# A band mask moved into the score product: sliding-window attention with an MLP gate on one Trainium2 core

## The chip, the cores and the metric

The kernel runs on one core of a Trainium2 chip. The core has five engines with queues of their own: PE (TensorE, matrix products, with a separate row PEld for its weight loads), ACT (ScalarE), DVE (VectorE), POOL (GpSimd) and SP (SyncE, which here only issues DMAs). The metric is the device time of one execution in microseconds; lower is better.

## The reference, cut to what matters

`S` = 2048 tokens, `D` = 512, 32 heads of width 16. Each token attends to itself and to the seven tokens at distances 2, 4, ..., 14 before it.

```python
xn = layernorm(x)
q, k, v = split(xn @ wqkv)                      # 32 heads of 16
off = arange(8) * 2                             # W = 8, dil = 2
idx = pos[:, None] - off[None, :];  mask = idx >= 0
logits = einsum("bhsd,bhswd->bhsw", q, k[idx]) * 16 ** -0.5
attn = softmax(where(mask, logits, -1e9))
s = einsum("bhsw,bhswd->bhsd", attn, v[idx]).reshape(B, S, D) @ wo
h = gelu(layernorm(xn) @ w1);  x1 = xn + shift_groups(h) @ w2
g = silu(x1 + gelu(layernorm(x1) @ w3) @ w4)
out = xn + s * g
```

## The kernel before

A distance of 2 between keys keeps even and odd tokens apart. The kernel splits the sequence into two parities `p` of `M` = 1024 tokens; within one, a query sees itself and the 7 keys before it, a band of width 8.

**The stages ahead** (0 to about 110 us) are layer norm, transposes, `q`, `k`, `w1`, `w2` and `w3`. They leave `qm` (queries, with a copy that keeps the even heads and one that keeps the odd ones), `kT`, `xnT` and the hidden activations `h3`.

**The attention loop** runs over 18 units `n`: 9 per parity (`NU` = 9), the first with 128 queries, seven with 120, the last with 56; each has its queries' keys plus the 8 before. Per unit:

- `scores(p, u, dd)`, twice: two PSUM tiles `s_ps` (`jj` = 0, 1). A tile takes four products of K = 32 rows and 2 x 120 columns; the row group of the array is `r = 64 * jj + 32 * b`, and `b` also picks the bank of the tile. ACT takes the exponential of a whole tile into `prob` (line 407). Then one DVE multiplication sets everything outside the band to zero (line 409, `mask0` or `mask1`).
- `weighted(p, u, ...)` of the unit before: 32 products of 32 columns' width into `o_ps`, values in half of the rows and the softmax sums in the other half. `o_ps` is copied to two tiles `orw`, one copy by ACT (line 439), one by DVE (line 441).
- `values` of the next unit: four products into `v_ps`, copied by DVE to `v_aug`.
- `fill[n]`: other PE work put between the two calls of `scores` (`fill[n][0]`) and behind them (`fill[n][1]`). It holds halves of the `w4` product: a tile `w_ps` is 9 or more products in two halves (5, then 6 and one by the identity), then ACT's tanh `sig` and a DVE step into `xn`.

PSUM: three buffers `psA` (for `s_ps` and `o_ps`, five allocations a unit, taken in turn) and two buffers `psB` (for `v_ps`, `w_ps` of w4, `wo_ps`). PE's order in the loop is the program's (`pin`).

**The softmax division** is done for several units at once, a *run*: 4, 3 and 2 units in each parity, written here (p, r). After a run's last unit `normalise(p, r)` sends the sums from `orw` to DRAM (`den_d`), reads them back spread over 128 partitions (`dn`), takes the DVE reciprocal `rb` (line 468), writes it (`rden_d`) and reads it back repeated over the heads (`rr`, four DMAs); all these DMAs stand on SP's queue. Eight DMAs on POOL's queue bring the values into `oT`. Later `normalise_end(p, r)` multiplies `oT` by `rr` on DVE (line 480). Each engine works its own queue in order, so a DVE instruction that waits for a DMA holds up all behind it.

**The end**: `final_tile(p, i)` multiplies 128 tokens of `oT` by `wo` (`wo_ps`), gates by `xn`, adds to the input `xo` (loaded by `load_xo`) and sends pairs of tiles out. Before, all 16 final tiles stand behind the loop.

Of the kernel before, what the change touches and what calls it, by code (L numbers as in the profile page):

```python
# [15 lines left out]
def kernel(  # L16
# [31 lines left out]
    NQ = 120  # L48

# [23 lines left out]
    sm5 = ctx.enter_context(tc.tile_pool(name="sm5", bufs=4))  # L73
# [59 lines left out]
    for i in range(16):  # L133
# [10 lines left out]
    mask0 = const.tile([P, P], BF16, name="mask0")  # L144
    nc.gpsimd.affine_select(
        out=mask0, in_=ones_bf[:], pattern=[[1, P]], compare_op=ALU.is_ge, fill=0.0,
        base=0, channel_multiplier=-1,
    )
    nc.gpsimd.affine_select(
        out=mask0, in_=mask0[:], pattern=[[-1, P]], compare_op=ALU.is_ge, fill=0.0,  # L150
        base=W - 1, channel_multiplier=1,
    )
    mask1 = const.tile([P, NQ], BF16, name="mask1")
    nc.gpsimd.affine_select(
        out=mask1, in_=ones_bf[:, 0:NQ], pattern=[[1, NQ]], compare_op=ALU.is_ge, fill=0.0,
        base=W, channel_multiplier=-1,
    )
    nc.gpsimd.affine_select(
        out=mask1, in_=mask1[:], pattern=[[-1, NQ]], compare_op=ALU.is_ge, fill=0.0,
        base=-1, channel_multiplier=1,  # L160
    )
# [225 lines left out]
    def scores(p, u, dd):  # L387
        q0, nq, k0, nk = units[u]
        msk = mask0 if u == 0 else mask1
        pr = sm4.tile([P, H * P // 2], BF16, name="prob", tag="s4")  # L390
        prv = pr[:, 0 : H * nq // 2].rearrange("p (t b x) -> p t b x", t=2, b=2)
        for jj in range(2):
            st = psa("s_ps")
            for dl in range(2):
                for b in range(2):
                    r = 64 * jj + 32 * b
                    dt = 2 * dd + dl
                    pin(
                        nc.tensor.matmul(  # L399
                            st[:nk, b, dl * 2 * nq : (dl + 1) * 2 * nq].rearrange("k (e q) -> k e q", e=2),  # L400
                            lhsT=kT[p][r : r + 32, dt, k0 : k0 + nk],
                            rhs=qm[p][r : r + 32, dt, :, q0 : q0 + nq],
                            start=True, stop=True, tile_position=(r, 0),
                        )
                    )
            with tc.issue_after(last["gelu"].ins):
                nc.scalar.activation(prv[:nk, jj], st[:nk, :, 0 : 4 * nq], AF.Exp, scale=SCALE)  # L407
        ph = pr[:, 0 : 16 * nq].rearrange("p (h q) -> p h q", q=nq)
        nc.vector.tensor_tensor(  # L409
            out=ph[:nk], in0=ph[:nk],  # L410
            in1=msk[:nk, 0:nq].unsqueeze(1).to_broadcast([nk, 16, nq]), op=ALU.mult,
        )
        return pr

    def weighted(p, u, va, prs):
# [3 lines left out]
        if u == runs[p][r][0]:  # L419
            orw[p] = [sm5.tile([P, ND, RW], BF16, name="orw", tag="s5") for jj in range(2)]  # L420
# [14 lines left out]
        for jj in range(2):  # L435
            dst = orw[p][jj][:, :, q0 - ra : q0 - ra + nq]
            src = op[:, jj, 0 : 4 * nq].rearrange("p (s q) -> p s q", q=nq)
            if jj == 0:
                nc.scalar.activation(dst, src, AF.Copy)  # L439
            else:  # L440
                nc.vector.tensor_copy(out=dst, in_=src)  # L441
# [5 lines left out]
    def normalise(p, r):  # L447
# [11 lines left out]
        for jj in range(2):  # L459
            for cg in range(4):  # L460
# [4 lines left out]
                )  # L465
        rb = small.tile([P, n], BF16, name="rb", tag="rb", bufs=1)
        with nc.allow_low_precision("bf16 weights"):
            nc.vector.reciprocal(out=rb, in_=dn)
        nc.sync.dma_start(out=rden_d.rearrange("h (a m) -> (h a) m", a=P // H), in_=rb)
        rr = sm5.tile([P, ND, RW], BF16, name="rr", tag="s5")  # L470
# [7 lines left out]
    def normalise_end(p, r):  # L478
        _, _, ra, rw = runs[p][r]
        nc.vector.tensor_tensor(  # L480
            out=oT[p][:, :, ra : ra + rw], in0=oT[p][:, :, ra : ra + rw], in1=rrs[p, r][:, :, 0:rw], op=ALU.mult
        )
# [3 lines left out]
    def load_xo(p):  # L486
        xo[p] = midt([P, M // P, D], f"xo{p}")
        nc.sync.dma_start(out=xo[p], in_=xv[p].rearrange("(i q) d -> q i d", q=P))
# [21 lines left out]
    stage_a1(0)  # L510
    stage_ln(1)
# [21 lines left out]
    NH = 28  # L533
    fill = {n: ([], []) for n in range(2 * NU)}
# [3 lines left out]
    fill[6][1].append(lambda: load_xo(0))  # L538
    fill[10][1].append(lambda: load_xo(1))
    fill[7][1].append(lambda: normalise_end(0, 0))  # L540
    fill[10][1].append(lambda: normalise_end(0, 1))
    fill[12][1].append(lambda: normalise_end(0, 2))
    fill[16][1].append(lambda: normalise_end(1, 0))
# [3 lines left out]
    for n, (p, u) in enumerate(order):  # L547
# [9 lines left out]
        if n + 1 < len(order):  # L557
            va = values(*order[n + 1])
    for h in halves[NH : NH + 2]:
# [42 lines left out]
```

## Time and profile before

| | us |
|---|---|
| median of 3 runs (lowest, highest) | 243.67 (242.24, 245.29) |
| the profiled execution: time | 244.33 |
| the profiled execution: span from first to last instruction | 242.6 |
| PE busy | 213.3 (88%) |
| DVE busy | 152.0 (63%) |
| ACT busy | 136.1 (56%) |
| POOL busy | 43.0 (18%) |

The span's 1.7 us less than the time lie before its first and behind its last instruction. The matrix products of a busy PE overlap, and their ends are modelled, so PE's share is an upper bound. Rows of the timeline give the start, the length, engine, line, operation, tiles and shapes, and in brackets the idle time ahead of the instruction with the instruction that ended it. Rows of the waits give the total, the number and the longest.

### The profile page before, as it was taken

Reading aid. Unit: us, or ns where it says so; the run is one execution under the profiler, and the core shown is the slowest. Engines: PE = TensorE matmul, PEld = TensorE weight load, DVE = VectorE, ACT = ScalarE, POOL = GpSimd, SP = SyncE. Lnnn points to the kernel's source line nnn. Section 1 sums busy time; section 2 is a strip of 40 time slices with the busy share of each in tenths; the row PEclk is TensorE's granted clock in tenths of the full one; section 3 lists DMA queues with packets and bytes.
Section 4 is the critical chain, followed back from the end, with each engine's and each line's share of the span. In section 5 each row is a group of like instructions: output and inputs, shape, how many; then the busy total and the mean of one; then the engine's idle time right before and its main releaser. Section 6 shows DMA issues by size and latency. Waiting matters only on the chain.

```text
span 242.6 us, 4350 instructions
## 1 busy us (share of the span) xinstructions
PE 213.3 (88%) x1720; PEld 93.2 (38%) x1720; DVE 152.0 (63%) x277; ACT 136.1 (56%) x164; POOL 43.0 (18%) x90
## 2 busy tenths in 40 slices
PE   8789999999999999999788983998797897699892
PEld 2335545444444444443333331343332333243330
DVE  6789965082596820003688746688686776837994
ACT  2083766738226165559889884568766978431000
POOL 2522440002022020000000420062300230426000
PEclk9999999999999999999999998699979999889999
DMA  5999200002406724000000290242700143223352
GB/s 171 356 378 351 78 0 3 0 0 86 86 3 165 181 87 89 0 1 0 3 0 3 23 242 10 82 70 55 221 18 17 16 81 90 32 43 92 116 174 90
DMA packets 28788, 21.31 MB, mean 88 GB/s; under 512 B 12672, under 2 KB 27744, under 8 KB 28768
## 3 DMA queue, kind: packets, MB, share of 16 engines
q1 hardware_dynamic: 25056, 16.85, 23.8%
q0 software_dynamic: 1536, 2.10, 4.8%
q10 hardware_dynamic: 2176, 2.10, 2.5%
q8 instruction: 13, 0.21, 0.4%
q14 instruction: 7, 0.06, 0.1%
HBM read 12.39 MB, written 4.46 MB: 69 GB/s over the span
## 4 chain that ended last, share of the span: by engine, by line
PE 48%; DMA 18%; DVE 13%; ACT 7%; issue 5%; SPq 5%; POOL 2%; DVEq 0%; ACTq 0%
PE w_ps L326 15%; PE qk_ps L249 9%; ACT prob L407 6%; PE w_ps L293 6%; PE w_ps L265 6%; PE w_ps L350 5%; SPq L472 3%; DVE prob L409 3%; DMA xn_85<-in_A_x_dram 3%; DMA dn<-den_d_1417 3%; PE v_ps L377 2%; DMA dn<-den_d_1877 2%; PE wo_ps L494 2%; PE s_ps L399 1%; DMA rr<-rden_d_1418 1%
## 5 line engine op out<-in xcount | busy, mean ns | idle before, releaser
L407 ACT ACTIVATE prob<-s_ps 128x960 bf16<-128x960 f32 (+2 forms) x72 | 62.5, 930 | 20.0 <-PE s_ps L399 19.9
L350 PE MATMUL w_ps<-w_sb,h3T 128*128 128x512 bf16 (+1 forms) x176 | 46.5, 403 | 3.2 <-DVE xn_85 L359 2.4
L409 DVE TENSOR_TENSOR prob<-prob,mask_145 128x1920 bf16<-128x1920 bf16 (+1 forms) x32 | 34.5, 1085 | 10.8 <-ACT prob L407 10.6
L326 PE MATMUL w_ps<-x1nT,w_sb 128*128 128x512 bf16 (+1 forms) x176 | 38.3, 379 | 0.0
L331 ACT ACTIVATE h3T<-w_ps 128x1024 bf16<-128x1024 f32 x20 | 20.5, 1023 | 25.6 <-PE w_ps L326 23.3
L326 PEld LDWEIGHTS <-w_sb 128*128 128x128 bf16 (+1 forms) x176 | 17.6, 100 | 20.4
L462 POOL DMA_DIRECT2D oT_1416<-orw x24 | 12.3, 522 | 73.4 <-ACT orw L439 73.2
L350 PEld LDWEIGHTS <-h3T 128*128 128x128 bf16 (+1 forms) x176 | 15.8, 101 | 24.3 <-issue 11.4
L382 DVE CAST v_aug_148<-v_ps 128x512 bf16<-128x512 f32 (+1 forms) x9 | 6.1, 683 | 23.3 <-PE v_ps L377 23.3
L462 POOL DMA_DIRECT2D oT_2229<-orw x24 | 12.1, 512 | 38.9 <-ACT orw L439 38.0
L249 PEld LDWEIGHTS <-wqk_sb 128*128 128x128 bf16 x128 | 12.1, 98 | 12.8
L249 PE MATMUL qk_ps<-xnT_152,wqk_sb 128*128 128x512 bf16 x64 | 15.4, 379 | 0.8 <-DVE xnT_152 L224 0.8
L255 ACT ACTIVATE qm_156<-qk_ps,hmask 128x1024 bf16<-128x1024 f32 x8 | 8.4, 1112 | 12.2 <-PE qk_ps L249 12.2
L358 ACT ACTIVATE sig<-w_ps 128x512 bf16<-128x512 f32 x16 | 9.8, 610 | 9.4 <-PE w_ps L356 9.4
L265 PE MATMUL w_ps<-xn2T,w_sb 128*128 128x512 bf16 x64 | 14.6, 379 | 0.0
L249 PE MATMUL qk_ps<-xnT_153,wqk_sb 128*128 128x512 bf16 x64 | 14.5, 379 | 0.0
L399 PE MATMUL s_ps<-qm_156,kT_154 32*128 32x240 bf16 (+2 forms) x144 | 8.8, 271 | 6.2 <-DVE orw L441 5.7
L298 DVE TENSOR_TENSOR xn_85<-w_ps,xn_85 128x1024 bf16<-128x1024 f32 x4 | 4.9, 1216 | 14.8 <-PE w_ps L293 14.8
L377 PE MATMUL v_ps<-wv_sb,xnT_153 128*128 128x512 bf16 (+1 forms) x36 | 9.9, 399 | 3.6 <-DVE xn_86 L359 3.6
L399 PE MATMUL s_ps<-qm_157,kT_155 32*128 32x240 bf16 (+2 forms) x144 | 9.2, 265 | 3.6 <-ACT prob L407 2.4
L255 ACT ACTIVATE qm_157<-qk_ps,hmask 128x1024 bf16<-128x1024 f32 x8 | 8.3, 1114 | 6.1 <-PE qk_ps L249 6.1
L441 DVE CAST orw<-o_ps 128x480 bf16<-128x480 f32 (+2 forms) x18 | 10.9, 625 | 0.0
(109 smaller groups left out, 281.7 us busy)
## 6 DMA issues: line engine op xcount, KB each, us to landing
w_sb<-in_B_w_dram SPq DMA_DIRECT2D x1, 1376.0 KB
w_sb<-in_B_w_dram SPq DMA_DIRECT2D x1, 1280.0 KB
wqk_sb<-in_A_wqkv_dram SPq DMA_DIRECT2D x2, 512.0 KB
w_sb<-in_B_w_dram SPq DMA_DIRECT2D x2, 512.0 KB
xn_86<-in_A_x_dram SPq DMA_DIRECT2D x4, 256.0 KB
xo_1566<-in_A_x_dram SPq DMA_DIRECT2D x1, 1024.0 KB
xo_1949<-in_A_x_dram SPq DMA_DIRECT2D x1, 1024.0 KB
out_dram<-xo_1566 ACTq DMA_DIRECT2D x4, 256.0 KB
```

Source lines behind the costliest of these rows:

```text
L249: nc.tensor.matmul(pt[:, b, :], lhsT=wqk_sb[:, dt, nt * P : (nt + 1) * P], rhs=xnT[p][:, dt, cs], start=(dt == 0), stop=(dt == ND - 1),)
L255: nc.scalar.activation(qm[p][:, 2 * a : 2 * a + 2, e, cs], pt, AF.Copy, scale=hmask[:, e : e + 1])
L265: nc.tensor.matmul(pt[:, b, :], lhsT=w1_sb[:, dt, g * P : (g + 1) * P], rhs=xn2T[:, dt, :], start=(dt == 0), stop=(dt == ND - 1),)
L293: nc.tensor.matmul(pt[:, j, :], lhsT=w2_src(p, g, m0), rhs=w2_sb[:, g, :], start=(g == 0), stop=(g == ND - 1),)
L326: nc.tensor.matmul(pt[:fs, ft % 2, :], lhsT=w3_sb[:, dt, ft * P : ft * P + fs], rhs=x1nT[:, dt, :], start=(dt == 0), stop=(dt == ND - 1),)
L331: last["gelu"] = nc.scalar.activation(h3T[:, 2 * a : 2 * a + 2, :], pt, AF.Gelu_apprx_tanh)
L350: nc.tensor.matmul(pt, lhsT=h3[c][:fs, ft, jj * P : (jj + 1) * P], rhs=w4_sb[:fs, ft, :], start=(ft == 0), stop=False,)
L377: nc.tensor.matmul(vp[:nk, :], lhsT=xnT[p][:, dt, k0 : k0 + nk], rhs=wv_sb[:, dt, :], start=(dt == 0), stop=(dt == ND - 1),)
L399: nc.tensor.matmul(st[:nk, b, dl * 2 * nq : (dl + 1) * 2 * nq].rearrange("k (e q) -> k e q", e=2), lhsT=kT[p][r : r + 32, dt, k0 : k0 + nk ...
L407: nc.scalar.activation(prv[:nk, jj], st[:nk, :, 0 : 4 * nq], AF.Exp, scale=SCALE)
L409: nc.vector.tensor_tensor(out=ph[:nk], in0=ph[:nk], in1=msk[:nk, 0:nq].unsqueeze(1).to_broadcast([nk, 16, nq]), op=ALU.mult,)
L462: nc.gpsimd.dma_start(out=oT[p][DH * hh : DH * (hh + 1), :, ra : ra + rw], in_=orw[p][jj][32 * cg : 32 * cg + DH, :, 0:rw],)
```

## The change

The band mask is no longer multiplied into `prob`. In each score tile a product per bank comes first that writes 0 inside the band and a multiple of -32768 outside it, for four heads at once (4 x 120 columns, K = 32); the score products then add to it, and the exponential makes zeros of what is outside. Its factors `m_a` and `m_b` are built by 14 short GpSimd instructions in the first stage and copied to the other three row groups by six small DMAs.

The ACT copy of `o_ps` goes to DVE, so that DVE does both. Runs are of three units each. The reciprocal and what follows it become `normalise_mid`, called two units behind the run's end for most runs; `normalise_end` comes two units behind that. `load_xo` is cut in four. The 8 final tiles of the first parity move into the loop, whose share of w4 halves goes from 28 to 26; the last six halves stand behind the loop.

```diff
+    def build_mask():
+        ma, mb = m_a[0:32, :], m_b[0:32, :]
...
+        for g in range(1, 4):
+            nc.sync.dma_start(out=m_a[32 * g : 32 * g + 32, :], in_=ma)
+            nc.sync.dma_start(out=m_b[32 * g : 32 * g + 32, :], in_=mb)
...
         for jj in range(2):
             st = psa("s_ps")
+            for b in range(2):
+                r = 64 * jj + 32 * b
+                pin(
+                    nc.tensor.matmul(
+                        st[:nk, b, 0 : 4 * nq].rearrange("k (e q) -> k e q", e=4),
+                        lhsT=m_a[r : r + 32, ka : ka + nk],
+                        rhs=m_b[r : r + 32, 0:nq].unsqueeze(1).to_broadcast([32, 4, nq]),
+                        start=True, stop=False, tile_position=(r, 0),
+                    )
+                )
...
-                            start=True, stop=True, tile_position=(r, 0),
+                            start=False, stop=(dl == 1), tile_position=(r, 0),
...
-        nc.vector.tensor_tensor(
-            out=ph[:nk], in0=ph[:nk],
-            in1=msk[:nk, 0:nq].unsqueeze(1).to_broadcast([nk, 16, nq]), op=ALU.mult,
-        )
...
-            if jj == 0:
-                nc.scalar.activation(dst, src, AF.Copy)
-            else:
-                nc.vector.tensor_copy(out=dst, in_=src)
+            nc.vector.tensor_copy(out=dst, in_=src)
...
+    def normalise_mid(p, r):
...
+            pin(nc.vector.reciprocal(out=rb, in_=dn))
         nc.sync.dma_start(out=rden_d.rearrange("h (a m) -> (h a) m", a=P // H), in_=rb)
...
+    for i in range(M // P):
+        m = 26 + i * 10 // 8
+        fill[m // 2][m % 2].append(lambda i=i: final_tile(0, i))
...
-    for cuts in ((0, 4, 7, NU), (0, 4, 7, NU)):
+    for cuts in ((0, 3, 6, NU), (0, 3, 6, NU)):
...
+        (5, lambda: normalise_mid(0, 0)), (7, lambda: normalise_end(0, 0)),
+        (8, lambda: normalise_mid(0, 1)), (10, lambda: normalise_end(0, 1)),
+        (10, lambda: normalise_mid(0, 2)), (12, lambda: normalise_end(0, 2)),
+        (14, lambda: normalise_mid(1, 0)), (16, lambda: normalise_end(1, 0)), (17, lambda: normalise_mid(1, 1)),
...
+    weighted(*prev)
     for h in halves[NH : NH + 2]:
         h()
-    weighted(*prev)
-    for h in halves[NH + 2 :]:
+    normalise_end(1, 1)
+    for h in halves[NH + 2 : NH + 4]:
         h()
-    for i in range(M // P):
-        final_tile(0, i)
-    normalise_end(1, 1)
-    for i in range(6):
+    normalise_mid(1, 2)
+    for h in halves[NH + 4 :]:
+        h()
+    for i in range(5):
         final_tile(1, i)
     normalise_end(1, 2)
-    for i in range(6, M // P):
+    for i in range(5, M // P):
```

On DVE in the middle of the first parity, around the first run's reciprocal. Before (in `rb_1431<-dn_1421` the division of run (0,0)):

```order
L359 SCALAR_TENSOR_TENSOR xn0_85<-sig_1486,w4_ps_1459 128x512
L382 CAST v_aug0_148<-v_ps_1526 128x32x16
L468 RECIPROCAL rb_1431<-dn_1421 128x122
L409 TENSOR_TENSOR prob_1532<-prob_1532,mask1_145 128x1920
L409 TENSOR_TENSOR prob_1552<-prob_1552,mask1_145 128x1920
L441 CAST orw_1490<-o_ps_1491 128x4x120
```

The same place on DVE after the change, where that division is `rb_1577<-dn_1387`:

```order
L460 CAST orw_1453<-o_ps_1455 128x4x120
L460 CAST orw_1454<-o_ps_1455 128x4x120
L399 CAST v_aug1_147<-v_ps_1490 128x32x16
L460 CAST orw_1453<-o_ps_1536 128x4x120
L460 CAST orw_1454<-o_ps_1536 128x4x120
L399 CAST v_aug0_145<-v_ps_1571 128x32x16
L493 RECIPROCAL rb_1577<-dn_1387 128x92
L376 SCALAR_TENSOR_TENSOR xn0_85<-sig_1611,w4_ps_1530 128x512
```

The mask multiplications are gone, each `o_ps` has two copies on DVE, and two units' copies (`o_ps_1455`, `o_ps_1536`) now stand ahead of the reciprocal of a run that ended with the unit before them.

On PE, one score tile after the change (before, the four `L426` products and their loads stood alone, and the tile of the other `jj` followed them):

```order
L414 LDWEIGHTS m_a_143
L414 MATMUL s_ps_1130<-m_b_144,m_a_143 128x480
L414 LDWEIGHTS m_a_143
L414 MATMUL s_ps_1130<-m_b_144,m_a_143 128x480
L426 LDWEIGHTS kT0_151
L426 MATMUL s_ps_1130<-qm0_153,kT0_151 128x240
L426 LDWEIGHTS kT0_151
L426 MATMUL s_ps_1130<-qm0_153,kT0_151 128x240
```

Two products of 480 columns now lead the tile; two more pairs of `L426` rows like the last two close it.

On SP's queue at the end of the program, the DMAs of the last two runs, before:

```order
L469 DMA rden_d11_2501<-rb_2514 128x90
L472 DMA rr_2517<-rden_d11_2501 128x1x360 x4
L455 DMA den_d12_2654<-orw_2566 4x4x176
L455 DMA den_d12_2654<-orw_2567 4x4x176
L458 DMA dn_2658<-den_d12_2654 128x44
L469 DMA rden_d12_2655<-rb_2668 128x44
```

and after:

```order
L494 DMA rden_d11_2580<-rb_2788 128x90
L474 DMA den_d12_2831<-orw_2656 4x4x296
L474 DMA den_d12_2831<-orw_2657 4x4x296
L497 DMA rr_2791<-rden_d11_2580 128x1x360 x4
L477 DMA dn_2835<-den_d12_2831 128x74
L494 DMA rden_d12_2832<-rb_2878 128x74
```

The four `rr` DMAs of run (1,1) now stand between the last run's two steps `den_d12` and `dn` instead of ahead of both, and the last run is 296 tokens wide instead of 176.

More of the change, by code (lines that the diff above doesn't have):

```diff
@@ L419, in weighted @@
         if u == runs[p][r][0]:
-            orw[p] = [sm5.tile([P, ND, RW], BF16, name="orw", tag="s5") for jj in range(2)]
+            orw[p] = [sm3.tile([P, ND, RW], BF16, name="orw", tag="s3") for jj in range(2)]
         op = psa("o_ps")
@@ L465, in normalise @@
                 )
+        rrs[p, r] = (dn, rden_d)
+    def normalise_mid(p, r):
+        _, _, ra, rw = runs[p][r]
+        n = H * rw // P
+        dn, rden_d = rrs[p, r]
         rb = small.tile([P, n], BF16, name="rb", tag="rb", bufs=1)
         with nc.allow_low_precision("bf16 weights"):
-            nc.vector.reciprocal(out=rb, in_=dn)
+            pin(nc.vector.reciprocal(out=rb, in_=dn))
         nc.sync.dma_start(out=rden_d.rearrange("h (a m) -> (h a) m", a=P // H), in_=rb)
-        rr = sm5.tile([P, ND, RW], BF16, name="rr", tag="s5")
+        rr = sm3.tile([P, ND, RW], BF16, name="rr", tag="s3")
         for dt in range(ND):
@@ L479, in normalise_end, with load_xo @@
         _, _, ra, rw = runs[p][r]
-        nc.vector.tensor_tensor(
-            out=oT[p][:, :, ra : ra + rw], in0=oT[p][:, :, ra : ra + rw], in1=rrs[p, r][:, :, 0:rw], op=ALU.mult
+        pin(
+            nc.vector.tensor_tensor(
+                out=oT[p][:, :, ra : ra + rw], in0=oT[p][:, :, ra : ra + rw], in1=rrs[p, r][:, :, 0:rw],
+                op=ALU.mult,
+            )
         )
     xo = {}
-    def load_xo(p):
-        xo[p] = midt([P, M // P, D], f"xo{p}")
-        nc.sync.dma_start(out=xo[p], in_=xv[p].rearrange("(i q) d -> q i d", q=P))
+    def load_xo(p, k):
+        if k == 0:
+            xo[p] = midt([P, M // P, D], f"xo{p}")
+        nc.sync.dma_start(
+            out=xo[p][:, 2 * k : 2 * k + 2, :],
+            in_=xv[p, 2 * k * P : (2 * k + 2) * P, :].rearrange("(i q) d -> q i d", q=P),
+        )
     def final_tile(p, i):
@@ L510 @@
     stage_a1(0)
+    build_mask()
     stage_ln(1)
@@ L532 @@
     halves = [h for w in w4s for h in w]
-    NH = 28
-    fill = {n: ([], []) for n in range(2 * NU)}
+    NH = 26
+    fill = {n: ([], [], []) for n in range(2 * NU)}
     for i in range(NH):
```

61 lines of the change are left out of this document (34 added, 27 removed).

## The prediction

> **What bounds the kernel now.** I read the stretches first, to see which engine limits which stage. Columns: the stretch in us, its length, busy time and instructions of PE, PEld, DVE, ACT and POOL, then the granted PE clock and the DMA share.
>
> ```profile
> 40.00:60.00 20.00, 20.00 (x95) 9.04 (x93) 7.07 (x15) 13.47 (x15) 1.26 (x2) 1.00 0.07 24
> 120.00:130.00 10.00, 9.17 (x125) 3.80 (x123) 7.43 (x9) 8.92 (x13) 0.00 (x0) 1.00 0.00 0
> 140.00:150.00 10.00, 6.41 (x101) 2.67 (x100) 4.64 (x7) 7.05 (x10) 1.29 (x3) 0.98 0.58 147
> 150.00:160.00 10.00, 8.41 (x73) 3.10 (x73) 7.58 (x10) 4.68 (x7) 1.32 (x3) 0.68 0.19 56
> ```
>
> Ahead of the loop PE is the bound without a gap, and the change leaves that alone. In the loop no engine is full: PE, ACT and DVE wait for each other in turn, and between 140 and 160 us all three stand still in part and the clock falls to 0.68. Next the waits, to see who holds whom:
>
> ```profile
> PE s_ps L399 <- DVE orw L441: 6.8, 5, 4.1
> DVE rb L468 <- DMA dn<-den_d_1417: 4.4, 1, 4.4
> PE v_ps L377 <- DVE xn_86 L359: 3.6, 2, 2.2
> PE s_ps L399 <- ACT prob L407: 2.8, 5, 1.1
> DVE oT_1416 L480 <- DMA rr<-rden_d_1878: 2.5, 1, 2.5
> ```
>
> and the timeline for the largest (start, length, engine, what; idle before in brackets):
>
> ```profile
> 147.81 0.92 DVE L468 RECIPROCAL rb<-dn 128x122 bf16<-128x122 bf16 x1 [4.41 <-DMA dn<-den_d_1417]
> 151.42 0.58 PE L399 MATMUL s_ps<-qm_156,kT_154 32*128 32x240 bf16 x4 [4.07 <-DVE orw L441]
> ```
>
> The reciprocal waits 4.41 us for its DMA at the head of DVE's queue; the `o_ps` copies behind it are late, no `s_ps` buffer comes free, and PE stands 4.07 us. So the loop is bound by DVE's queue waiting for DMAs, and elsewhere by ACT and DVE returning buffers. PE's own work gives the floor. One unit without a gap shows its prices:
>
> ```profile
> 125.22 0.60 PE L428 MATMUL o_ps<-prob,v_aug_150 128*32 128x120 bf16 x32
> 125.75 1.04 PE L377 MATMUL v_ps<-wv_sb,xnT_152 128*128 128x512 bf16 x4
> 126.72 0.39 PE L399 MATMUL s_ps<-qm_156,kT_154 32*128 32x240 bf16 x8
> 127.05 1.47 PE L350 MATMUL w_ps<-w_sb,h3T 128*128 128x512 bf16 x6
> 128.35 0.38 PE L356 MATMUL w_ps<-xn_85,ident 128*128 128x512 bf16 x1
> 128.67 0.39 PE L399 MATMUL s_ps<-qm_156,kT_154 32*128 32x240 bf16 x8
> 128.99 1.25 PE L350 MATMUL w_ps<-w_sb,h3T 128*128 128x512 bf16 x5
> 130.17 0.60 PE L428 MATMUL o_ps<-prob,v_aug_148 128*32 128x120 bf16 x32
> ```
>
> From start to start: `o_ps` 0.53, `v_ps` 0.97, a set of eight score products 0.33, a w4 tile 1.62 + 1.18 = 2.80. The loop's ends:
>
> ```profile
> 109.80 1.03 PE L377 MATMUL v_ps<-wv_sb,xnT_152 128*128 128x512 bf16 x4
> 217.48 0.39 PE L428 MATMUL o_ps<-prob,v_aug_150 64*32 64x56 bf16 x32
> 225.53 3.75 PE L494 MATMUL wo_ps<-wo_sb,oT_1416 128*128 128x512 bf16 x16 [0.73 <-DVE sg L500]
> ```
>
> From 109.80 to the end of the last `o_ps` at 217.8 are 108.0 us. PE's work in it: 15 w4 tiles x 2.80 = 42.0, 18 x 0.97 = 17.5, 36 sets x 0.33 = 11.9, 18 x 0.53 = 9.5, together 80.9. **27 us of the loop are lost**; this is what the change can win.
>
> **The change part by part.**
>
> *Work taken from DVE and ACT.* Busy us, mean ns and idle before:
>
> ```profile
> L409 DVE TENSOR_TENSOR prob<-prob,mask_145 128x1920 bf16<-128x1920 bf16 (+1 forms) x32 | 34.5, 1085 | 10.8 <-ACT prob L407 10.6
> L409 DVE TENSOR_TENSOR prob<-prob,mask_142 128x2048 bf16<-128x2048 bf16 x4 | 4.9, 1225 | 3.7 <-ACT prob L407 3.6
> L439 ACT ACTIVATE orw<-o_ps 128x480 bf16<-128x480 f32 (+2 forms) x18 | 10.0, 575 | 1.3 <-PE o_ps L428 1.3
> L358 ACT ACTIVATE sig<-w_ps 128x512 bf16<-128x512 f32 x16 | 9.8, 610 | 9.4 <-PE w_ps L356 9.4
> 122.70 3.56 ACT L407 ACTIVATE prob<-s_ps 128x960 bf16<-128x960 f32 x4 [0.66 <-PE s_ps L399]
> ```
>
> DVE loses 39.4 us and gets ACT's 18 copies, some 10 to 11 us. ACT's unit falls from 3.56 for four exponentials, 0.57 for the copy and 0.5 for `sig` (14 tiles of 0.61 over 18 units) to about 4.1 us; before, at about 4.7 of a 4.95 us unit, ACT was nearly the bound. Neither cut shortens PE's stream itself: their worth is that PE can run near its floor.
>
> *The mask products, which no row shows.* Each set gets four products of 480 columns, one per row group. Do the row groups run side by side? Score products alone in short stretches, with the number in flight:
>
> ```profile
> 128.66:128.68 0.02, 0.01 (x2) 1.00 0.00 0
> 128.68:128.70 0.02, 0.02 (x4) 1.00 0.00 0
> 128.78:128.80 0.02, 0.02 (x8) 1.00 0.00 0
> ```
>
> Four are in flight within 40 ns, the other four start 0.1 us later: two rounds of 0.1 us, and the rest of 0.33 us is the change to full products. 480 columns take two such rounds, so the likely price is +0.20 us a set: 36 x 0.20 = 7.2 us. The cheapest end is nothing, if the sets fit in PE's waits; the dearest is all four in turn, +0.8 us a set. In between, when the second tile's buffer is late, its two products run behind the first's: +0.4. I take 0.20, nearest to the rows. The Trainium skill, "TensorE: Matmul & The Clock Gate", section "The mechanism", says that matmuls start and end strictly in program order. By that rule a third product on a busy row group would hold the second tile back, and the price would be the 0.4. The row with four in flight at 128.68 speaks against it.
>
> *PE's new sum.* w4 13 tiles, 36.4; `wo` 8 tiles at 3.75 / 4 = 0.94, 7.5; 17.5; 36 x 0.53 = 19.1; 9.5. Together 90.0 us.
>
> *The waits that stay.* The reciprocal and the `oT` product now stand two units, about 10 us, behind what they wait for. The waits above cost PE 6.8 us at `s_ps` and the low clock; they go, except at run (0,2), where `normalise_mid` follows after one unit and `xo` loads stand on SP ahead of its `dn`. There DVE may stand 1 to 2 us; behind it wait `sig` steps and copies that PE needs only 4 us later. What is late next: in a unit with only one w4 half the exponentials are. Without the first half (units 5 and 7) the fourth score tile needs the first's exponential, which ends some 1.5 us after the unit's start (0.53 for the set, 0.1 to start, 0.89 for one exponential), while PE is there at 0.5: 1.0 us each. Without the second half (1, 3, 10, 12) the next unit's second tile needs the fourth exponential: about 0.6 each. In units 13 to 16 `psB` carries w4, `wo` and `v` together, and a buffer returns only after `sig` and DVE: 0.5 each. With 1.6 for the loop's start and DMAs that makes 2.0 + 2.4 + 2.0 + 1.6 = **8 us**. As bounds: 3 us, if ACT runs ahead, and 17, if the two `o_ps` copies in a row on DVE, 1.2 us instead of 0.6, keep PE's buffers as late as now.
>
> The last `o_ps` thus ends at 109.8 + 90.0 + 8 = 207.8, 10 us earlier.
>
> *The tail.* Copies, SP issue, reciprocal, and from the chain of waits the last product, tiles and copy:
>
> ```profile
> 218.82 0.95 DVE L441 CAST orw<-o_ps 128x480 bf16<-128x480 f32 x2
> 221.12 1.12 SPq L455 DMA_DIRECT2D den_d_2654<-orw  x2
> 228.07 0.42 DVE L468 RECIPROCAL rb<-dn 128x44 bf16<-128x44 bf16 x1
> 235.41 0.53 DVE oT_2229 L480
> 235.99 1.97 PE wo_ps L494 x8
> 238.67 0.33 DVE xo_1949 L501
> ```
>
> From the copies' end at 219.77 to the span's end are 22.8 us. Up to the reciprocal I take the same 8.3: the four `rr` issues of run (1,1), 2.5 us of SP, delay this run's DMAs on either side of `den_d`. A run of 296 instead of 176 tokens adds 0.2 to the reciprocal and 0.3 to the product, and three tiles hang on it instead of two, +1.1: in all +1.6. PE then has 13 us of work (three w4 tiles, five `wo`) for a wait of about 16. A gap like that can halve the clock:
>
> ```profile
> 209.65 1.02 PE L377 MATMUL v_ps<-wv_sb,xnT_153 128*64 128x512 bf16 x4 [2.15 <-DVE xn_86 L359]
> 210.83 2.56 PE L350 MATMUL w_ps<-w_sb,h3T 128*128 128x512 bf16 x6
> ```
>
> After 2.15 us of idling six products took 2.56 instead of 1.47. Three tiles at half clock cost about 1.5 more; I take half, 0.7. The same page of the Trainium skill, section "HAM oscillation — how this bites in real kernels", puts the limit at idle gaps over 3.4 us. By that the gap would be free; the row shows a drop after less.
>
> Copies end at 207.8 + 0.95 = 208.8, and the span at 208.8 + 22.8 + 1.6 + 0.7 = 233.9, against 242.6: **-8.7 us**. The mask's preparation costs nothing: POOL and SP stand idle where it falls.
>
> ```profile
> POOL l1r L179 <- DVE l1m L187: 20.0, 4, 6.6
> SPq L306 <- DVE xn_619 L302: 38.3, 1, 38.3
> ```
>
> Without that cover it would be 14 instructions of at most 0.3 us, 4 us.
>
> The profiled execution took 244.33, so by it 235.6; its time lies 0.66 above the median of the runs. From the median: 243.67 - 8.7 = **235.0**.
>
> **The rivals.**
>
> *A: the mask products run tile by tile* (+0.4 a set). For it: a wait between the two tiles makes it so even with free row groups. Against it: the four in flight. 7.2 us more: 242.2, within 2%.
>
> *B: the loop stays bound by the return of buffers.* Three `psA` buffers serve five allocations a unit, and DVE now does both `o_ps` copies. With 17 us lost instead of 8 the time is 244. For it: ACT and DVE held PE in every stretch of the loop. Against it: both have less to do, and 4.1 us of ACT stand against 5 us of PE in a unit.
>
> *C: slower, as the mask products run one by one.* At +0.8 a set they cost 29 us instead of 7.2: 256.6. It decides from about +0.58 a set on (235.0 + 36 x 0.38 = 248.7). For it: nobody has shown four 480-column products with the same factor. Against it: two rounds in 0.33 us.
>
> *D: the waits all but vanish and the clock stays up:* 3 us lost, no 0.7: 229.3.
>
> **How the numbers follow.** Forecast 0.57, D 0.14, A 0.12, B 0.11, C 0.06. All that this measurement can tell from no change is some 2%, 238.8 to 248.5. The forecast and D lie below it, less a little of the forecast's upper side: faster 0.70, same 0.23, slower 0.07. The range runs from D with some room, 227, into A and B, 243; C and the upper part of B stay out.
>
> **What the profile after would show.** Sets of twelve products in 0.53 us; the `L409` rows gone and no reciprocal or `oT` row in the loop with over 2 us of idling for a DMA; the last `o_ps` near 207.8; PE idle about 3 us before the last three tiles; PEclk at 9 up to there. It is wrong if sets take 0.7 or more, if PE's waits for `prob` or `orw` grow to 15 us, or if the tail exceeds 25 us by much.

## The result and the profile after

The changed kernel took 236.71 us (median of 4 runs, 234.50 to 239.16) beside 244.44 of the kernel before in the same rounds; the ratio is 0.967 (95% interval 0.956 to 0.978). Run again in a later set it gave 236.09 us (235.19 to 237.38) and 0.970 (0.964 to 0.976). The prediction was 235.0 with a range of 227 to 243.

The profiled execution took 236.67 us with a span of 234.9. Cut at the first `v_ps` of the loop and at the end of the last `o_ps`, the two kernels compare as follows. The view is that of the stretches, with the columns of the prediction's first fence and GB/s at the end; here before:

```profile
109.80:217.90 108.10, 90.08 (x1118) 36.85 (x1117) 74.30 (x93) 79.05 (x106) 20.42 (x40) 0.94 0.24 56
```

and after:

```profile
111.40:207.90 96.50, 91.84 (x1253) 40.62 (x1269) 52.18 (x88) 70.64 (x88) 20.50 (x40) 1.00 0.27 69
207.90:234.90 27.00, 16.76 (x73) 6.79 (x68) 14.77 (x28) 1.79 (x3) 4.05 (x8) 0.90 0.30 88
```

| stretch of the profiled execution, us | before | predicted | after |
|---|---|---|---|
| start of the loop | 109.8 | 109.8 | 111.4 |
| loop | 108.1 | 98.0 | 96.5 |
| end of the last `o_ps` to the end | 24.7 | 26.1 | 27.0 |
| span | 242.6 | 233.9 | 234.9 |

PE is now busy for 91.84 of the loop's 96.50 us at full clock; DVE and ACT have room. The four largest of the waits that PE still has in the loop (110 to 205 us), which add up to 3.7 us:

```profile
PE s_ps L414 <- ACT prob L434: 0.7, 1, 0.7
PE s_ps L414 <- DVE orw L460: 0.7, 1, 0.7
PE wo_ps L526 <- DVE v_aug_145 L399: 0.6, 1, 0.6
PE v_ps L394 <- DVE sg L532: 0.5, 2, 0.2
```

The 6.8 us behind `orw` have become 0.7. The reason is on DVE's timeline around the first run's division:

```profile
142.89 0.68 DVE L399 CAST v_aug_145<-v_ps 128x512 bf16<-128x512 f32 x1
143.49 0.72 DVE L493 RECIPROCAL rb<-dn 128x92 bf16<-128x92 bf16 x1
```

No bracket stands behind the reciprocal, so it waited for nothing; before, that row carried 4.41 us. In the whole loop DVE now waits for a DMA at one reciprocal (0.9 us) and at one `oT` product (0.4 us). A whole set on PE, and one whose second tile came late:

```profile
119.75 0.40 PE L414 MATMUL s_ps<-m_b,m_a 32*128 32x480 bf16 x4
119.97 0.39 PE L426 MATMUL s_ps<-qm_153,kT_151 32*128 32x240 bf16 x8
120.28 0.63 PE L450 MATMUL o_ps<-prob,v_aug_145 128*32 128x128 bf16 x32
...
121.82 0.38 PE L414 MATMUL s_ps<-m_b,m_a 32*128 32x480 bf16 x2
122.03 0.37 PE L426 MATMUL s_ps<-qm_153,kT_151 32*128 32x240 bf16 x4
122.26 0.38 PE L414 MATMUL s_ps<-m_b,m_a 32*128 32x480 bf16 x2
122.46 0.38 PE L426 MATMUL s_ps<-qm_153,kT_151 32*128 32x240 bf16 x4
122.77 0.61 PE L367 MATMUL w_ps<-w_sb,h3T 128*128 128x512 bf16 x2
```

The whole set takes 120.28 - 119.75 = 0.53 us, as predicted; the split one 0.95. 28 of the 36 sets are whole and 8 split. In the program each tile's two mask products are followed by its own four score products; in the whole set the mask products of both tiles start first. So the second tile's products started ahead of score products that precede them in the program, and the strict order that the prediction weighed did not hold here.

### The profile page after: what moved, and what is told of

Its sections match the earlier page's. It is cut to its first block, busy times and chain, and to the rows that moved or that the text cites. A ratio compares the mean times of both kernels' runs of the same rounds, so it can differ in the third digit from the quotient of the medians.

```text
span 234.9 us, 4562 instructions
## 1 busy us (share of the span) xinstructions
PE 213.9 (91%) x1835; PEld 96.7 (41%) x1864; DVE 125.7 (54%) x259; ACT 127.9 (54%) x146; POOL 46.5 (20%) x100
## 4 chain that ended last, share of the span: by engine, by line
PE 69%; DVE 10%; ACT 7%; DMA 4%; issue 3%; POOL 3%; SPq 1%; DVEq 0%; ACTq 0%
PE w_ps L343 16%; PE w_ps L367 10%; PE qk_ps L266 10%; PE w_ps L310 6%; PE w_ps L282 6%; PE v_ps L394 5%; PE wo_ps L526 5%; ACT prob L434 5%; PE s_ps L414 4%; PE s_ps L426 3%; PE o_ps L450 2%; DVE sg L532 2%; DVE orw L460 2%; DMA rr<-rden_d_2580 2%; DMA xn_85<-in_A_x_dram 1%
## 5 line engine op out<-in xcount | busy, mean ns | idle before, releaser
L434 ACT ACTIVATE prob<-s_ps 128x960 bf16<-128x960 f32 (+2 forms) x72 | 62.4, 930 | 24.7 <-PE s_ps L426 24.6
L367 PE MATMUL w_ps<-w_sb,h3T 128*128 128x512 bf16 (+1 forms) x172 | 42.4, 380 | 0.8 <-DVE xn_85 L376 0.3
L460 DVE CAST orw<-o_ps 128x480 bf16<-128x480 f32 (+2 forms) x36 | 21.1, 622 | 7.7 <-PE o_ps L450 7.7
L367 PEld LDWEIGHTS <-h3T 128*128 128x128 bf16 (+1 forms) x176 | 15.1, 97 | 19.7 <-issue 5.1
L414 PE MATMUL s_ps<-m_b,m_a 32*128 32x480 bf16 (+2 forms) x144 | 16.7, 362 | 1.4 <-ACT prob L434 0.7
L266 PEld LDWEIGHTS <-wqk_sb 128*128 128x128 bf16 x128 | 12.4, 100 | 13.4 <-issue 1.1
L266 PE MATMUL qk_ps<-xnT_149,wqk_sb 128*128 128x512 bf16 x62 | 16.7, 402 | 0.9 <-DVE xnT_149 L241 0.8
L376 DVE SCALAR_TENSOR_TENSOR xn_85<-sig,w_ps 128x512 bf16<-128x512 bf16 x8 | 5.5, 688 | 22.1 <-ACT sig L375 22.1
L266 PE MATMUL qk_ps<-xnT_150,wqk_sb 128*128 128x512 bf16 x63 | 14.4, 379 | 0.1
L526 PE MATMUL wo_ps<-wo_sb,oT_2241 128*128 128x512 bf16 x31 | 9.0, 440 | 5.3 <-DVE xn_86 L376 2.7
L414 PEld LDWEIGHTS <-m_a 32*128 32x128 bf16 (+1 forms) x144 | 4.9, 92 | 17.4 <-issue 14.4
```

Source lines behind the costliest of these rows:

```text
L266: nc.tensor.matmul(pt[:, b, :], lhsT=wqk_sb[:, dt, nt * P : (nt + 1) * P], rhs=xnT[p][:, dt, cs], start=(dt == 0), stop=(dt == ND - 1),)
L367: nc.tensor.matmul(pt, lhsT=h3[c][:fs, ft, jj * P : (jj + 1) * P], rhs=w4_sb[:fs, ft, :], start=(ft == 0), stop=False,)
L414: nc.tensor.matmul(st[:nk, b, 0 : 4 * nq].rearrange("k (e q) -> k e q", e=4), lhsT=m_a[r : r + 32, ka : ka + nk], rhs=m_b[r : r + 32, 0:nq ...
L526: nc.tensor.matmul(pt, lhsT=oT[p][:, dt, i * P : (i + 1) * P], rhs=wo_sb[:, dt, :], start=(dt == 0), stop=(dt == ND - 1),)
```

## The experiments

"Theory" means here: the loop of before lost its time to DVE standing at the head of its queue for the division's DMAs; the later steps end that, and the products and the lighter DVE let PE run near its floor. All runs in one table (ratio to the kernel before on the same chip; the expected time is that of the first theory in each text):

| kernel | median us | ratio (95% interval) | expected us |
|---|---|---|---|
| changed, first set | 236.71 | 0.967 (0.956 to 0.978) | 235.0 |
| e1 products only | 251.23 | 1.033 (1.026 to 1.041) | 249 |
| e2 changed, multiplies back | 241.04 | 0.992 (0.989 to 0.996) | 236.5 |
| e3 changed, preparation late | 236.53 | 0.975 (0.970 to 0.979) | 235.1 |
| e4 changed, products twice | 241.85 | 0.995 (0.991 to 0.999) | 244 |
| e5 changed again | 236.09 | 0.970 (0.964 to 0.976) | 235 to 236 |
| e6 order alone | 236.71 | 0.971 (0.966 to 0.976) | 238 |
| e7 changed, ACT copies back | 236.06 | 0.968 (0.961 to 0.975) | within 1 of changed |
| e8 tail filled | 234.37 | 0.963 (0.957 to 0.968) | 229 |
| e9 tail filled, den by ACT | 234.83 | 0.967 (0.963 to 0.971) | 228.5 |
| e10 later steps only | 233.82 | 0.963 (0.959 to 0.967) | 233 |
| e11 order, runs of 4, 3, 2 | 235.04 | 0.970 (0.965 to 0.974) | 236 |
| e12 later steps and products | 237.08 | 0.974 (0.968 to 0.980) | 233.8 |

### The two halves: products without the order, the order without products (e1, e2)

e1 is the kernel before with the products, and the preparation of their factors, alone:

```diff
+                nc.tensor.matmul(st[:nk, b, ...], lhsT=m_a[...], rhs=m_b[...], start=True, stop=False)
-                            start=True, stop=True, tile_position=(r, 0),
+                            start=False, stop=(dl == 1), tile_position=(r, 0),
-        nc.vector.tensor_tensor(out=ph[:nk], in0=ph[:nk], in1=msk..., op=ALU.mult)
```

> The kernel before with the mask products alone: no DVE multiply, all else (order of the softmax-sum steps, runs, fill, ACT's half of the o_ps copies) as before. Theory 1, the loop of before lost its time to DVE standing in the reciprocal and the oT product until their DMAs landed: those waits stay, the 36 sets cost PE 7.2 us more, only the waits of PE on the multiplies (about 2 us) go: 244 + 7 - 2 = 249 us (246 to 252). Rival 2, the multiply between the exponential and the weighted sums was the loss: about 238 us. If the mask rows' preparation costs the first stage 1.6 us, the loop starts at about 111.4 here too, else at 109.8.

It took 251.2 us: slower by 8, inside the first theory's range (246 to 252). Its waits of DVE between 110 and 206 us show why freeing DVE did not help:

```profile
DVE rb L487 <- DMA dn<-den_d: 13.8, 4, 4.5
DVE oT L499 <- DMA rr<-rden_d: 11.4, 3, 4.8
```

With less to do, DVE reaches the division's steps earlier and stands there longer: 25 us, where the same rows of the kernel before add up to 12 in the same stretch (the two largest, 4.4 and 2.5, stand in the prediction). The loop of e1, and the row of its tail that holds PE up:

```profile
110.20:220.10 109.90, 94.14 (x1244) 41.31 (x1261) 36.35 (x56) 78.89 (x106) 20.50 (x40) 0.95 0.23 55
```

```profile
227.97 0.91 DVE L499 TENSOR_TENSOR oT<-oT,rr 128x1440 bf16<-128x1440 bf16 x1 [3.25 <-DMA rr<-rden_d]
229.87 5.30 PE L513 MATMUL wo_ps<-wo_sb,oT 128*128 128x512 bf16 x16 [3.81 <-DVE sg L519]
```

The profiled execution's span is 6.7 us longer than before, and the place differs from the theory: 0.4 us lie in the start, 1.8 in the loop and 4.5 in the tail. In the loop PE was busy for 4.1 us more and stood still for 2.3 less, so the waits took up part of the products. In the tail DVE stood for a division's DMA again, and PE behind it.

e2 is the reverse edit in the changed kernel: both masks and the 36 multiplies back, no products, all else as changed.

> The changed kernel with the two bf16 masks and the 36 DVE multiplies back in the place of the products; order, runs, fill and both copies on DVE as changed. Theory 1, the order of the softmax-sum steps brings the gain: the loop's PE work falls by 7.2 us to about 85 us, but DVE's rises from 52 by 39 to about 92 us, so the loop is bound by DVE and takes about 98 us instead of 96.6, and the first stage gets its 1.6 us back: about 236.5 us (234 to 240). Rival 2, the products are what opens the loop: 242 us or more.

241.0 us, against an expected 236.5. Its loop:

```profile
109.80:211.70 101.90, 84.87 (x1108) 36.29 (x1125) 88.62 (x124) 70.70 (x88) 20.40 (x40) 1.00 0.26 65
```

DVE is busy for 89 us where I had worked out 92, but the loop takes 101.9, not 98: DVE is busy 87% of it, and PE stands still for 17 us, 14 of them behind steps of DVE. Most of the gain over before was gone, so the second theory of e2, that the products open the loop (242 us or more), seemed the nearer one at this point. It was not, as e6 shows.

### The preparation of the mask (e3, e5)

```diff
-    build_mask()          # behind stage_a1(0)
+    with tc.issue_after(last["pow"].ins):   # the last square root of stage_ln(3)
+        build_mask()
```

> The changed kernel with the preparation of the mask's rows held behind the last reciprocal square root of the four first layer norms on POOL; all else as changed. Theory 1, the selects between chunk 0's reciprocal square roots delay the first stage by 1.6 us: the loop starts at 109.8 instead of 111.4 us and the time is 1.5 us less than the changed kernel's, 235.1. Rival 2, the delay comes from the landing of the first x rows or the clock of that execution: start and time as in the changed kernel.

> The changed kernel again, beside the kernel before in the same rounds, since its first interval was wide (0.956 to 0.978). Theory, the profiled execution's late loop start (111.4 us) was partly the clock: executions with the first products of the projections at full clock start the loop at about 110.3, as two kernels with the same mask preparation did, and take 235 to 236 us; ratio 0.970. Rival, the preparation always costs 1.6 us: the loop starts at 111.4 again.

e3's loop started at 110.11 and e5's, with the preparation where the change puts it, at 110.17. The first rows of the loop in e3 and in e5:

```profile
110.11 1.03 PE L394 MATMUL v_ps<-wv_sb,xnT 128*128 128x512 bf16 x4
```

```profile
110.17 1.03 PE L394 MATMUL v_ps<-wv_sb,xnT 128*128 128x512 bf16 x4
```

So the preparation did not cost the 1.6 us that the first profile after suggested. Kernels with the old masks started at 109.69 to 110.12, the others with the preparation in the first stage (e1, e4, e7, e12) at 110.12 to 110.48: some 0.3 to 0.4 us by their means, with one profiled execution of each. About 0.35 us more of the first execution's delay came with an `x` tile that landed later (its first transposes began at 8.42 us, those of e5 at 8.07). The rest, 0.9 us by difference, goes with its clock. In the stretch 10 to 15 us of that execution, and of e5's:

```profile
10.00:15.00 5.00, 3.80 (x14) 1.57 (x14) 3.73 (x11) 0.08 (x1) 3.51 (x10) 0.66 1.10 350
```

```profile
10.00:15.00 5.00, 4.14 (x22) 1.89 (x22) 4.47 (x12) 1.82 (x2) 3.16 (x9) 1.00 1.10 349
```

At 0.66 PE did 14 products in that stretch, at full clock 22. e3's time, 236.53, is that of the changed kernel.

### The price of the products (e4)

```diff
-            for b in range(2):
+            for rep, b in ((0, 0), (0, 1), (1, 0), (1, 1)):
...
-                        start=True, stop=False, tile_position=(r, 0),
+                        start=(rep == 0), stop=False, tile_position=(r, 0),
```

> The changed kernel with each mask product issued twice (the second adds the same mask again). Theory 1, four products of a set run side by side and PE sets the loop: +0.20 us for each of 36 sets, +7.2 us, about 244. Rival 2, part of it falls into PE's remaining 4.7 us of waits in the loop: +3 to +5 us. Rival 3, products of the two tiles follow each other in strict order: +0.4 us a set, +14 us, 251.

The loop of e4:

```profile
110.30:212.40 102.10, 98.58 (x1393) 45.68 (x1411) 52.18 (x88) 71.38 (x88) 20.41 (x40) 1.00 0.26 65
```

Against the changed kernel's 96.50 the loop grew by 5.6 us and PE's busy time by 6.7, which is 0.19 us for each of 36 sets. So the products of a set do run side by side, and 5.6 of the 6.7 us of PE's time are the loop's time. The median rose by 5.1 us: between the first theory (7.2) and the second (3 to 5). Rival 3, +14, is out.

### The order without the mask change (e6), and ACT's copies (e7)

e6 is the kernel before with every later step, the runs of 3, the fill and the tail of the change; mask and copies stay as before. e7 is the changed kernel with one edit:

```diff
-            nc.vector.tensor_copy(out=dst, in_=src)
+            if jj == 0:
+                nc.scalar.activation(dst, src, AF.Copy)
+            else:
+                nc.vector.tensor_copy(out=dst, in_=src)
```

> The kernel before with the order alone: the softmax-sum steps later and pinned, runs of 3, the fill and the tail as changed; the DVE multiplies stay and ACT makes its half of the o_ps copies as before. In the loop DVE then has 78 us (88.7 in the kernel with the multiplies back, less 11 for 18 copies), ACT 81 and PE 85. Theory 1, PE waited behind DVE's full queue, so taking 11 us from DVE gives back a good part of the 4 to 5 us that the multiplies cost: about 238 us (236.5 to 239.5). Rival 2, the multiply's place between exponential and weighted sums is what costs, whatever DVE's load: 241. Rival 3, the products bring nothing over the old masks: 236.5 or less.

> The changed kernel with the first of each two o_ps copies back on ACT. In the loop ACT goes from 71 to 81 us, DVE from 52 to 41, PE stays at 92 of 96.6. Theory 1, both engines have room and PE sets the loop: within 1 us of the changed kernel. Rival 2, the copy stands in ACT's queue ahead of an exponential for which PE waits (ACT holds the score buffers): 2 to 4 us slower.

236.71 and 236.06 us. e6 lies at the lower end of its first theory (236.5 to 239.5), and that theory's mechanism holds: against e2, freeing DVE of 11 us gave back 4.3. It also bears out what rival 3 says, though not its time (236.5 or less): the order alone is as fast as the whole change in the same rounds (236.09), and where ACT keeps its copies the masks on DVE cost nothing that can be measured (0.971 and 0.968, with overlapping intervals). Executions with the same mean clock of 0.989 took 235.2 to 235.3 us in e5 and 236.4 to 237.1 in e6, so some 1 us in favour of the whole change is not excluded. The loops of e6 and of e7:

```profile
109.70:208.60 98.90, 85.50 (x1126) 36.30 (x1125) 80.77 (x108) 78.14 (x105) 20.49 (x40) 1.00 0.27 67
```

```profile
110.10:205.90 95.80, 93.00 (x1269) 40.62 (x1268) 43.91 (x71) 78.02 (x104) 20.50 (x40) 1.00 0.28 69
```

With the multiplies PE has 7.5 us less to do and waits 13.4 us instead of 2.8. So the products shorten the loop by 3.1 us; in these two executions e7's start is 0.4 and its tail 2.0 us longer, with a lower clock in the tail (0.83 against 0.92), which leaves the two about even. And ACT's ten microseconds of copies matter to nobody once PE sets the pace: e7 says that moving them was free, e2 against e6 that moving them **without** taking the multiplies from DVE costs 4 us.

### Which part of the order (e10, e11, e12)

e10 takes one step from the change, the later division: reciprocal and `rr` come one or two units later, the `oT` products up to one, and both DVE steps are pinned. Runs, copies, masks and output tiles stay as before.

```diff
-            nc.vector.reciprocal(out=rb, in_=dn)       # in normalise
+            pin(nc.vector.reciprocal(out=rb, in_=dn))  # in normalise_mid
...
-    fill[7][1].append(lambda: normalise_end(0, 0))
...
+        (6, lambda: normalise_mid(0, 0)), (8, lambda: normalise_end(0, 0)),
+        (9, lambda: normalise_mid(0, 1)), (11, lambda: normalise_end(0, 1)),
+        (10, lambda: normalise_mid(0, 2)), (12, lambda: normalise_end(0, 2)),
+        (15, lambda: normalise_mid(1, 0)), (17, lambda: normalise_end(1, 0)), (17, lambda: normalise_mid(1, 1)),
```

> The kernel before with one part of the order alone: reciprocal, rden and rr rows split from the den rows and issued a unit or two later, pinned, and the oT products pinned at their old places (one unit later where the run's rows come later); masks on DVE, runs of 4, 3 and 2 units, output tiles of the first half in the tail, all as before. Theory 1, DVE standing for DMAs was the loop's loss and this removes it: the loop falls from 108 to about 96 us, the tail stays at 25, about 233 us (231 to 236), no worse than the whole order with its output tiles in the loop. Rival 2, the shorter runs and the output tiles in the loop are a good part of the gain: 238 to 241.

> The kernel before with the order of the changed kernel (later steps, output tiles of the first half in the loop, tail, loads in quarters) but runs of 4, 3 and 2 units; masks on DVE, ACT copies. Theory, the runs' length matters only in the tail, where a last run of 2 units leaves 2 output tiles behind the last oT product instead of 3: about 236 us, 0 to 1 us under the order with runs of 3. Rival, with four buffers of 488 columns instead of five of 368 the rr rows wait for buffers: 238 to 240.

e10 took 233.8 us, the lowest median of all. Its first division on DVE's timeline:

```profile
146.63 1.16 DVE L409 TENSOR_TENSOR prob<-prob,mask 128x1920 bf16<-128x1920 bf16 x1 [0.66 <-ACT prob L407]
147.71 0.65 DVE L441 CAST orw<-o_ps 128x480 bf16<-128x480 f32 x1
148.28 0.68 DVE L382 CAST v_aug<-v_ps 128x512 bf16<-128x512 f32 x1
148.87 0.91 DVE L474 RECIPROCAL rb<-dn 128x122 bf16<-128x122 bf16 x1
```

The reciprocal runs 1.06 us later than before (147.81), and the multiply, copy and `v_aug` that used to stand behind it are done ahead of it. The division was never urgent; only its place in the queue was wrong. The loop and the tail of e10:

```profile
110.10:205.20 95.10, 84.52 (x1118) 35.69 (x1117) 72.36 (x91) 78.99 (x107) 20.40 (x40) 0.98 0.26 64
205.20:233.50 28.30, 17.88 (x82) 7.17 (x76) 21.31 (x41) 1.19 (x3) 4.04 (x8) 0.97 0.34 103
```

The loop loses 13.0 us and the tail, with all 16 output tiles in it, gains 3.6. Of the 13.0 us, 7.4 are time in which PE stood still (18.0 before, 10.6 now), and 5.6 are PE's busy time for the same 1118 instructions, as its granted clock rose from 0.94 to 0.98. e11 (the order with output tiles in the loop, runs as before) took 235.0, between e10 and e6; the intervals of the three overlap or touch (e10 up to 0.967, e11 from 0.965, e6 from 0.966), so shorter runs and the output tiles' place brought nothing that can be measured, and by the medians cost 1 to 3 us.

e12 puts the products into e10:

> The kernel with the later steps alone, and the mask products in the place of the DVE multiplies: the fourth corner of old and later steps by multiplies and products (ACT copies, runs of 4, 3 and 2, output tiles of the first half in the tail in all four). Theory, the products cost PE 7.2 us in the loop and take as much of PE's waits behind DVE: within 2 us of 233.8 (232 to 235.5). Rival 2, PE's 87 us of the loop's 95 leave no waits to win back: 240, as with the old steps, where the products cost 8 us. Rival 3, the multiplies hold the loop once DVE stands no more: 230 or less.

237.1 us, 0.974 (0.968 to 0.980), above e10's 0.963 (0.959 to 0.967) by more than both intervals. This closes a square (median us, in brackets the ratio to before):

| | multiplies on DVE | products on PE |
|---|---|---|
| old steps | 243 to 244 (1) | 251.2 (1.033) |
| later steps only (e10, e12) | 233.8 (0.963) | 237.1 (0.974) |
| whole order, ACT copies (e6, e7) | 236.7 (0.971) | 236.1 (0.968) |

The products cost 8 us where DVE stands for DMAs (more of it in the tail than in the loop, as e1 showed), 3 with the later steps, and nothing that can be measured in the whole order. In e12's loop PE is busy for 6.8 us more than in e10's and the loop only 0.8 longer:

```profile
110.50:206.40 95.90, 91.35 (x1262) 39.52 (x1261) 35.20 (x55) 79.01 (x107) 20.43 (x40) 1.00 0.26 63
206.40:236.00 29.60, 19.42 (x80) 7.61 (x76) 21.40 (x41) 1.19 (x3) 4.04 (x8) 0.93 0.32 98
```

The expected 233.8 was missed by 3 us, and so was rival 2's 240. The remaining 1.7 us of span lie in the start (0.4) and in the tail (1.3), where sixteen `wo` products took 5.30 us instead of 3.75. The tail's 1.3 go with its clock (0.93 against 0.97 in the last columns above). That is not the whole difference of the medians: executions with a mean clock of 0.996 took 235.81 us in e12 and 233.75 and 233.90 in e10, so by these few executions some 2 us stay with the products.

### A shorter tail (e8, e9)

In the changed kernel's tail, SP and DVE at the last two runs:

```profile
210.16 1.16 SPq L474 DMA_DIRECT2D den_d_2831<-orw  x2
211.62 2.50 SPq L497 DMA_DIRECT2D rr<-rden_d_2580  x4
214.24 0.38 SPq L477 DMA_DIRECT2D dn<-den_d_2831  x1
```

```profile
217.34 0.91 DVE L506 TENSOR_TENSOR oT_2241<-oT_2241,rr 128x1440 bf16<-128x1440 bf16 x1 [2.69 <-DMA rr<-rden_d_2580]
218.17 0.61 DVE L493 RECIPROCAL rb<-dn 128x74 bf16<-128x74 bf16 x1
226.34 0.78 DVE L506 TENSOR_TENSOR oT_2241<-oT_2241,rr 128x1184 bf16<-128x1184 bf16 x1
```

The last run's `dn` stands behind the `rr` rows of the run before. e8 takes the late preparation of e3, and puts `normalise_mid(1, 1)` one unit earlier and five output tiles of the first parity behind the loop (their places are told in a comment here):

```diff
-(17, lambda: normalise_mid(1, 1))
+(16, lambda: normalise_mid(1, 1))
...
+    final_tile(0, 3)      # and 4 to 7, between and behind the last w4 tiles
```

> The changed kernel with the mask preparation late, five output tiles of the first half taken from the loop's last units into the tail (between the last three gate tiles), and the reciprocal of the second half's middle run one unit earlier, in the loop, so that the last run's den row comes through SP's queue about 3 us sooner. Theory 1, PE sets the loop and the last run's DMA chain sets the tail, in which PE stood for 5 us: the loop loses 4.3 us of PE work, the tail loses its idle time and the half clock behind it: about 229 us (227 to 232). Rival 2, the loop is held by ACT or by DVE's queue once PE has less to do there: the loop keeps its 96.6 us, about 234.

e9 adds to it, and issues the `oT` product of run (1,1) after the last w4 tile:

```diff
+            q = nc.scalar if (p, r) == (1, 2) else nc.sync
+            q.dma_start(out=hv[jj], in_=orw[p][jj][DH : P : 32, :, 0:rw])
```

> The kernel with the filled tail, in whose tail the last run's den rows stood 3 us in SP's queue behind the rr rows of the run before (issued at 206.8 us, the copies done at 203.6): now ACT's queue issues them, and the oT product of the run before comes after the last gate tile. Theory, PE has work to the end: 202.3 (last o_ps) + 19.2 us of PE work + 4.9 from the last product to the end = 226.4, and about 228.5 us in all (227 to 230). Rival, the DMA chain of the last run still sets the end: oT ready at 221 instead of 224.6, about 231.

234.4 and 234.8 us: both expectations missed by 5 to 6 us. e8's loop and tail:

```profile
110.10:202.30 92.20, 88.43 (x1250) 38.45 (x1249) 48.27 (x79) 70.53 (x88) 20.50 (x40) 1.00 0.27 66
202.30:232.40 30.10, 20.27 (x91) 8.35 (x88) 18.57 (x36) 1.79 (x3) 4.05 (x8) 0.98 0.31 96
```

The loop fell by 4.3 us, as expected, and the tail grew by 3.1. An output tile costs DVE about 1.05 us (0.68 and 0.37) against 0.94 of PE, so the moved tiles fill DVE's queue: in e9 the last run's `rr` issues were over at 216.07, but its product came at 223.71, behind the steps of eight output tiles that stand ahead of it in the queue; it waited for no DMA:

```profile
222.67 0.75 DVE L534 TENSOR_TENSOR xo<-sg,xo 128x512 bf16<-128x512 bf16 x2
223.71 0.78 DVE L507 TENSOR_TENSOR oT<-oT,rr 128x1184 bf16<-128x1184 bf16 x1 [0.28 <-issue]
```

I had counted PE and the DMAs for the tail and left DVE out of the sum. Neither is measurably faster than e10, which stays the simplest version: faster than before, and by medians 2 to 3 us under the changed kernel, though the intervals of those two still touch (0.967 and 0.964).

## Why the prediction was right, and where it was not

**The loss and its place: right.** The prediction took the division's waits at the head of DVE's queue, above all the reciprocal's 4.41 us and what stands behind it, for the loop's main loss. e10 removes just these waits, and the loop falls from 108.1 to 95.1 us; e1 leaves them, and is slower than before. The 27 us that the prediction called lost were 18.0 us in which PE stood still and 9.2 of PE's busy time beyond its sum (90.08 against 80.9), part of it at the low clock.

**The price of the products: right.** 0.53 us a set in the rows; 0.19 us for each doubled set in e4. Rival A (+0.4) came true in the 8 split sets of 36 alone; C (+0.8) is out, as is B: 96.5 - 90.0 = 6.5 us are lost in the loop, not 17. D's 3 us were not reached.

**The waits that stay: right in size, not in their parts.** 8 us were forecast over PE's sum and 6.5 found. But PE stood still for only 4.7 of them, 0.9 for exponentials where 2.0 + 2.4 were forecast; the other 1.8 are busy time that the sum had left out, such as the split sets.

**The worth of taking work from DVE and ACT: wrong.** This is the step that failed: "their worth is that PE can run near its floor", with ACT "nearly the bound". The sum has the right size for this kernel, since PE indeed runs near its floor. But the floor had been raised by 7 us to get there. e6, without products and without moved copies, waits 13.4 us over a PE sum of 85.5 and is as fast within what was measured; e7, with the copies back on ACT, is as fast too. I priced the whole change and never the later steps alone, which a sum over the same rows would have allowed.

**The mask's preparation: nearly.** "Costs nothing" against some 0.3 to 0.4 us. The other 1.2 of the 1.6 us in the profiled execution were a late `x` tile and its clock, which one profile alone could not have told.

**The tail: right in the sum, not in its parts.** Copies' end (210.25) to span's end: 24.65 against 25.1. The copies themselves ended 2.35 us behind the last `o_ps`, not 0.95. Forecast was one gap of 3 us ahead of the last three tiles, and half of a half-clock penalty. The last of these rows of PE has the gap, of 2.49 us; another one that I had not seen precedes it, as the `oT` product of run (1,1) held the last w4 tile's step on DVE:

```profile
215.68 1.02 PE L526 MATMUL wo_ps<-wo_sb,oT_2241 128*128 128x512 bf16 x4
219.37 5.30 PE L526 MATMUL wo_ps<-wo_sb,oT_2241 128*128 128x512 bf16 x15 [2.67 <-DVE xn_86 L376]
227.17 2.84 PE L526 MATMUL wo_ps<-wo_sb,oT_2241 128*128 128x512 bf16 x12 [2.49 <-DVE oT_2241 L506]
```

The fifteen slowed products lie on the chain of work that ended last: DVE's steps behind them stand ahead of the last `oT` product, which waited for no DMA. It started 8.2 us after the last run's reciprocal; in e6, where it did wait for the DMA, 7.4. So by estimate the slowed products cost up to 0.8 us. The last twelve ran at full speed. The sums for start, loop and tail missed by +1.6, -1.5 and +0.9 us, so the good total owes something to errors of opposite sign.

## What to carry to other kernels

A wait at the head of an in-order queue is removed by issuing the waiting instruction later, behind work that is ready; here that alone, with no arithmetic moved to another engine and the first reciprocal 1 us later, was worth 9 us. Moving work from an engine that has room only looks useful while the queue is blocked: it made the blocked engine wait longer (12 to 25 us in the same stretch), and the products gave PE some 7 us more to do (e12 against e10, e7 against e6). When a change has separable parts, price each alone, and count every engine in the stretch that work is moved into.

## What was not expected of the hardware

- In these traces the granted clock is full or half, and changes only in steps of 3.41 us, counted from its first rise in the trace. Over the 14 profiled executions, PE stood still for 2.0 us or more in 16 such steps at full clock, and each time the clock was halved from the step's end on. Of the 885 steps with less, 4 were followed by it (1.3 to 1.9 us). So the length of a gap alone does not tell: ahead of the last twelve products PE stood for 2.57 us both in e7 and in e5, but 2.27 and 1.81 us of it lay in one step. The products took 4.29 us in e7 and 2.84 in e5. Two steps of e7, then those of e5 (the granted clock is the third column from the end):

```profile
221.44:224.85 3.41, 1.14 (x5) 0.29 (x3) 2.92 (x6) 0.00 (x0) 0.00 (x0) 1.00 0.43 147
224.85:228.27 3.42, 3.12 (x8) 1.20 (x9) 1.36 (x3) 0.00 (x0) 0.00 (x0) 0.50 0.00 1
```

```profile
221.61:225.02 3.41, 1.60 (x8) 0.49 (x5) 2.81 (x7) 0.00 (x0) 0.00 (x0) 1.00 0.46 150
225.02:228.43 3.41, 2.65 (x12) 1.08 (x12) 2.24 (x4) 0.00 (x0) 0.00 (x0) 1.00 0.13 44
```

- Executions of one kernel differ along with their clock: in e5 those with a mean granted clock of 0.989 took 235.2 to 235.3 us, those of 0.972 to 0.983 236.9 to 237.4.
- A set whose second tile comes late runs its halves one after the other, 0.95 us instead of 0.53. That is what rival A priced; it happened in 8 of the 36 sets of the profiled execution.
